# Attention scores from scaled fp16 halves in two sets, prepared one job ahead

## The chip, the cores and the metric

The kernel runs on one core of a Trainium2 chip. Its time is the device time of one execution in microseconds (us). TensorE (PE, its weight loads PEld) multiplies matrices, VectorE (DVE), ScalarE (ACT) and GpSimd (POOL) work on elements, and SyncE (SP) and ScalarE issue the DMA transfers of this kernel. Operands lie in SBUF, on 128 partitions; matmul results lie in PSUM.

## The reference

Attention of 8 batches with 8 heads, 576 positions and 64 columns a head, with a causal mask and a bias that falls with the running sum of max(s, 0); then a feed-forward network on the 4608 rows of 512:

```python
scores = 1.0 / np.sqrt(D) * np.matmul(q, k.transpose(0, 1, 3, 2))
cum = np.cumsum(np.maximum(s, 0.0), axis=-1)
bias = -(cum[:, :, :, None] - cum[:, :, None, :])
scores = np.where(causal, -1e9, scores + np.minimum(bias, 0.0))
attn = np.exp(scores - np.max(scores, axis=-1, keepdims=True))
attn = attn / (np.sum(attn, axis=-1, keepdims=True) + 1e-09)
x = np.matmul(attn, v)                      # then heads beside each other: 4608 x 512
h = x @ w_in                                # 512 x 2048
g = np.where(h >= 1, h, np.where(h <= -1, 0.0, (h + 1) ** 2 / 4.0))
out = g @ w_out                             # 2048 x 512
```

q, k, v and s are float32, and w_in and w_out float64. Both matter to the kernel: the weights are turned into pairs of fp16 numbers on the chip, and q and k are 8 times larger than a plain draw of 0.1 would be.

## The kernel before, in words

**Jobs.** Attention is cut into 64 jobs, each with two heads of one batch (a pair) and one half of the queries. HALF 0 has queries 0 to 320 and HALF 1 the other 256. A batch is 8 jobs: four pairs with half 0, then four with half 1. `att_slot(j, k)` emits job j in eight slots. Slot 0 prepares the operands (`att_prep`), slots 2 to 7 hold the job's six score tiles (`scores`), slot 3 loads the next job's q and k (`att_load`), and slot 7 multiplies the weights of the job before with v (`att_out`).

**Score operands.** `att_load` brings q and k, transposed, twice each: rows 0 to 63 and 64 to 127 of the tiles rq and rk get the same 64 columns of the head (four DMAs on SP, one buffer each). `att_prep` makes Q1 and K1 (q and k rounded to fp32r, a shorter float that TensorE takes as an operand) and Q2 and K2. Rows 64 to 127 of Q1 and rows 0 to 63 of K2 hold what rounding left, so that two matmuls give hi*hi + lo*hi + hi*lo. Rows 64 to 67 of Q2 and K2 carry the running sums in two parts against constant ones: thus the bias comes out of the same matmul (KC = 68 rows). Those rows are written by DMA from cumd, a copy of the running sums in HBM. There is one tile of each, Q1, K1, Q2 and K2, so a job's operands can be written only after the last score of the job before has read them.

**A job's chain.** The two matmuls of a score tile (L385, L386) fill one of two PSUM buffers of the tag "s". L391 (VectorE) adds the mask and takes the row minimum (scores are held negated), L402 (ScalarE) takes the exponential and its sum, L418 and L419 make the reciprocal, L423 to L426 and L429 (POOL, ScalarE, VectorE) make two fp16 halves pb of the normalised weights, and L430 transposes pb by DMA on SP into pt. Then `att_out` runs L448, the matmuls px of v's halves with pt, into a buffer of the same tag "s", and L459 and L460 make the fp16 halves of x.

**Feed-forward.** For each batch and half, 16 blocks ft of 128 hidden columns: 12 matmuls h (L502), the activation on ScalarE, VectorE and POOL (L514, L517, L518, L528, L529), and 12 matmuls y (L541) two blocks later. Four blocks go with one attention job, and attention runs about one half-batch ahead of the network, which needs x of all four pairs. At a boundary of two batches, job 8b+7's px must be done before the network can go on, and job 8b+8's operands are prepared.

**Start.** The float64 weights are decoded in 16 pieces each (`Weights.decode`, L193 to L204; `split` makes fp16 halves, L220 to L230). Those of w_in are decoded beside jobs 0 to 3, each in the four slots k = 0, 2, 4, 6; those of w_out while the network's first 16 blocks h run. v is scaled per batch in `batch_start`.

**Order.** The program is written in the loop order above, but a scheduler puts the instructions of each engine into one fixed order when the kernel is built, by priorities and its own estimate of times; `tc.high_priority` moves the score's minimum, the activations and x forward, and `late` and `issue_after` hold back the second half of pb. On the chip each engine goes through its order and waits for what is not ready. POOL makes K2 in the first 12 jobs (K_POOL), VectorE in the others.

## Time and profile before

| | |
|---|---|
| median of 3 runs | 1176.75 us (1176.42 to 1180.47) |
| profiled execution | 1170.07 us, span 1168.3 us |
| mean granted TensorE clock | 0.961 |
| TensorE busy | 1010.3 us, 86% |
| VectorE busy | 881.0 us, 75% |
| ScalarE busy | 744.6 us, 64% |
| POOL busy | 685.6 us, 59% |
| DMA moved | 158.04 MB, mean 135 GB/s |

The page's slices show how the kernel goes through its stages (40 slices of 29.2 us, tenths of busy time):

```profile
PE   1334677599998999889998999899989999899998
DVE  8988976778777877778777877788768777787633
ACT  5665686567746775667647765777557774777533
PEclk9997997599998999999999999999998999899999
```

TensorE fills up in the first eight slices and is then nearly full, with a step to 8 about every fourth slice: one step a batch. To read the rows: L385 is line 385 of the kernel before; an arrow shows out<-in; a bracket gives the idle time of the engine just before, and what ended it. A matmul's duration overlaps the next one's, so that starts are what can be subtracted.

### The profile page before, as it was taken

The page shows a single profiled execution, that of the slowest core. Times are in us where ns is not written, and L with a number is a line of the kernel's source. Part 1 is how long each engine was busy: PE and PEld are TensorE (multiplying, and loading weights), DVE is VectorE, ACT ScalarE, POOL GpSimd, SP SyncE. Part 2 cuts the span into 40 slices and gives each one's busy share as a digit, 9 for nine tenths or more (in the row PEclk, how much of TensorE's full clock was granted, in tenths as well). Part 3 has the DMA queues.
Part 4 walks back from the last instruction along what each step waited for, and adds up shares of the span by engine and source line. Part 5 has one row for each costly group of instructions (what it writes and reads, how often), then busy time and mean ns, then how long its engine had stood idle before and what let it go on. Part 6 is the DMA issues. An engine that isn't in the chain of part 4 may idle for free. (4 is left out here: it accounts for less than half of the span.)

```text
span 1168.3 us, 25129 instructions
## 1 busy us (share of the span) xinstructions
PE 1010.3 (86%) x8470; PEld 780.1 (67%) x8470; DVE 881.0 (75%) x2403; ACT 744.6 (64%) x1719; POOL 685.6 (59%) x1169
## 2 busy tenths in 40 slices
PE   1334677599998999889998999899989999899998
PEld 0222455477776877677776877677768877787787
DVE  8988976778777877778777877788768777787633
ACT  5665686567746775667647765777557774777533
POOL 4775247776546655565547664675647654775522
PEclk9997997599998999999999999999998999899999
DMA  8885316677528663677438753766537753667300
GB/s 256 210 190 154 121 58 151 153 149 159 140 75 182 155 160 83 124 155 166 118 86 177 152 145 83 166 145 156 120 93 167 163 139 78 156 141 160 79 27 19
DMA packets 343081, 158.04 MB, mean 135 GB/s; under 512 B 291112, under 2 KB 324264, under 8 KB 342952
## 3 DMA queue, kind: packets, MB, share of 16 engines
q1 hardware_dynamic: 334024, 147.26, 55.3%
q10 hardware_dynamic: 8928, 9.18, 2.5%
q8 instruction: 67, 1.10, 0.4%
q14 instruction: 62, 0.51, 0.2%
HBM read 75.33 MB, written 9.73 MB: 73 GB/s over the span
## 5 line engine op out<-in xcount | busy, mean ns | idle before, releaser
L502 PE MATMUL h<-x,WI 128*128 128x256 f16 (+1 forms) x3072 | 448.6, 291 | 24.3 <-DVE u L518 17.0
L541 PE MATMUL y<-g,WO 128*128 128x256 f16 (+1 forms) x3072 | 450.7, 290 | 9.9 <-POOL g L529 5.2
L502 PEld LDWEIGHTS <-WI 128*128 128x128 f16 x3072 | 292.7, 99 | 118.0 <-issue 28.4
L541 PEld LDWEIGHTS <-WO 128*128 128x128 f16 x3072 | 287.3, 99 | 99.4 <-issue 15.1
L529 POOL TENSOR_TENSOR g<-u,g 128x320 f16<-128x320 f32 (+1 forms) x256 | 204.4, 798 | 204.0 <-ACT g L528 198.6
L514 ACT ACTIVATE u<-h,ub,us 128x320 f32<-128x320 f32 (+1 forms) x256 | 150.2, 587 | 183.0 <-PE h L502 165.3
L402 ACT ACTIVATE p<-p,mn 64x64 f32<-64x64 f32 (+4 forms) x320 | 178.8, 559 | 107.2 <-DVE mn L391 82.2
L423 POOL TENSOR_SCALAR pb<-p,rs 64x128 f16<-64x128 f32 (+4 forms) x160 | 104.7, 655 | 167.4 <-DVE rs L419 117.8
L517 DVE SCALAR_TENSOR_TENSOR h<-h,ws,u 128x320 f32<-128x320 f32 (+1 forms) x256 | 132.5, 519 | 80.2 <-ACT u L514 80.1
L391 DVE CUSTOM_DVE_ANT_0 p<-s,mask 64x64 f32<-64x64 f32 (+4 forms) x320 | 135.1, 423 | 74.4 <-PE s L386 68.4
L385 PE MATMUL s<-K,Q 128*128 128x288 f32 (+4 forms) x384 | 151.2, 396 | 41.1 <-DVE mn L391 26.6
L429 DVE SCALAR_TENSOR_TENSOR pb<-p,rs,pb 64x128 f16<-64x128 f32 (+4 forms) x160 | 134.5, 841 | 52.4 <-POOL pb L423 52.0
L426 POOL TENSOR_TENSOR pb<-p,pb 64x128 f16<-64x128 f32 (+4 forms) x160 | 166.0, 1038 | 8.4
L386 PE MATMUL s<-K,Q 68*128 68x288 f32 (+4 forms) x384 | 121.3, 319 | 25.3 <-DMA K<-cumd 19.0
L518 DVE SCALAR_TENSOR_TENSOR u<-u,r,h 128x320 f32<-128x320 f32 (+1 forms) x256 | 130.2, 510 | 7.7 <-DVE h L517 0.5
L424 ACT ACTIVATE p<-p,rs 64x64 f32<-64x64 f32 (+4 forms) x160 | 89.4, 560 | 61.0 <-DVE rs L419 58.5
L528 ACT CAST g<-u 128x320 f16<-128x320 f32 (+1 forms) x256 | 108.4, 423 | 14.7 <-DVE u L518 14.5
L385 PEld LDWEIGHTS s<-K,Q 128*128 128x128 f32 (+1 forms) x384 | 74.6, 195 | 62.5 <-DVE mn L391 35.7
L448 PE MATMUL px<-pt,vt 128*64 128x256 f16 (+3 forms) x1536 | 89.0, 264 | 22.8 <-DMA pt<-pb 13.5
L448 PEld LDWEIGHTS <-vt 128*64 128x64 f16 x1536 | 75.8, 116 | 45.3 <-issue 32.4
L386 PEld LDWEIGHTS s<-K,Q 68*128 68x128 f32 (+1 forms) x384 | 76.1, 199 | 28.7 <-ACT x L459 10.1
L425 POOL TENSOR_SCALAR pb<-p 64x128 f16<-64x128 f32 (+4 forms) x160 | 91.2, 570 | 4.6 <-ACT p L424 2.0
(116 smaller groups left out, 954.6 us busy)
## 6 DMA issues: line engine op xcount, KB each, us to landing
rk<-in_k_dram SPq DMA_DIRECT2D x64, 288.0 KB
rq<-in_q_dram SPq DMA_DIRECT2D x64, 160.0 KB
rk<-in_k_dram SPq DMA_DIRECT2D x64, 160.0 KB
v<-in_v_dram SPq DMA_DIRECT2D x32, 288.0 KB
wir<-in_moe_w_in_dram SPq DMA_DIRECT2D x16, 512.0 KB
rq<-in_q_dram SPq DMA_DIRECT2D x64, 128.0 KB
wor<-in_moe_w_out_dram SPq DMA_DIRECT2D x16, 512.0 KB
out_dram<-o ACTq DMA_DIRECT2D x32, 160.0 KB
```

The costliest lines, as they stand in the source:

```text
L385: T.matmul(sc[:R, :c1 - c0], Q1[:, hd, qo:qo + R], K1[:, hd, c0:c1], start=True, stop=False)
L386: T.matmul(sc[:R, :c1 - c0], Q2[:KC, hd, qo:qo + R], K2[:KC, hd, c0:c1], start=False, stop=True)
L391: ttr[0] = V.tensor_tensor_reduce(out=Pt[:R, c0:c1], in0=sc[:R, :c1 - c0], in1=mask[:R, mo:mo + c1 - c0], scale=1.0, scalar=3.0e38 if mn i ...
L402: A.activation(Pt[:R, :W], Pt[:R, :W], AF.Exp, bias=m2[:R], scale=-1.0, accum_out=sums[n, i][:R, hd:hd + 1])
L426: G.tensor_tensor(los[1], pw, his[1], ALU.subtract)
L429: V.scalar_tensor_tensor(los[0], pv, rs[:R, :1], his[0], ALU.mult, ALU.subtract)
L448: T.matmul(px[hd * D:(hd + 1) * D, lo:N], VT[:, vl * NB + j, hd * D:(hd + 1) * D], PT[:, 4 * j + 2 * hd + pl, lo:], start=(m == 0), stop=( ...
L502: T.matmul(h[:, :N], WI[4 * kt + ft // 4][:, wl, ft % 4 * P:(ft % 4 + 1) * P], x[:, kt, xl], start=(n == 0), stop=(n == 3 * NKT - 1),)
L514: first = A.activation(u, h[:, :N], AF.Relu, bias=ubi[b], scale=usc[b]).ins
L517: V.scalar_tensor_tensor(h[:, :N], h[:, :N], wsc[b], u, ALU.mult, ALU.max)
L529: G.tensor_tensor(g[:, 1], u, g[:, 0], ALU.subtract)
L541: T.matmul(ys[b, hf, m][:, :N], WO[8 * (m // 2) + ft // 2][:, wl, c0:c0 + P], g[:, gl], start=(ft == 0 and n == 0), stop=(ft == NFT - 1 an ...
```

## The change

The score operands become fp16, in two sets that alternate by job, and a job's operands are prepared in slot 5 of the job before. fp16 has a small range, so q, k and the running sums are scaled by powers of two. For the running sums the power comes from their largest value (ctop, once). For q and k it comes, per batch, from a bound on what they can hold: each row's sum of magnitudes, taken by ScalarE (`scan`, an Abs with an accumulator) over q and k of the coming batch, which eight more loads per batch bring in (`scan_load`, 128x576 float32 each, on SP); `qk_scale` then takes the maximum over partitions with two transposes on TensorE, works out the factors in one-column operations on VectorE, and spreads them to all partitions with a matmul. `L465` divides the scale out again when it adds the mask. The running sums have three fp16 parts instead of two fp32r ones (NL = 3, KC = 70), and the constant rows beside them hold the scales (qkc), written by DMA in the first two jobs of each batch. The DMAs of these rows move from SP's queue to ScalarE's. Where POOL made K2, ScalarE now scales rk first.

```diff
-    LOADQ, CUMQ, FIRSTQ = nc.sync, nc.sync, nc.sync
+    LOADQ, CUMQ, FIRSTQ, SCANQ = nc.sync, nc.scalar, nc.sync, nc.sync
...
-    KC = D + 4
+    NL = 3
+    KC = D + 2 * NL
...
-    Q1 = cp.tile([P, 2, NQ], F32R, name="Q1")
-    K1 = cp.tile([P, 2, S], F32R, name="K1")
-    Q2 = cp.tile([P, 2, NQ], F32R, name="Q2")
-    K2 = cp.tile([P, 2, S], F32R, name="K2")
+    SETS = [
+        tuple(cp.tile([P, 2, m], F16, name=f"{t}_{i}") for t, m in (("Q1", NQ), ("K1", S), ("Q2", NQ), ("K2", S)))
+        for i in range(2)
+    ]
...
+    def scan_load(b, p):
+        for t, src in enumerate((qT, kT)):
+            raw = scans[b, p, t] = ap.tile([P, S], F32, tag="scan", bufs=2, name=f"sc{b}_{p}_{t}")
+            SCANQ.dma_start(raw, src[b, 2 * p:2 * p + 2].rearrange("h d n -> (h d) n"))
+    def scan(b, p):
+        if p == 0:
+            qkp[b] = ap.tile([P, 2, NPAIR], F32, tag="qkp", name=f"qkp{b}")
+        for t in range(2):
+            raw = scans.pop((b, p, t))
+            A.activation(raw, raw, AF.Abs, accum_out=qkp[b][:, t, p:p + 1])
+    def qk_scale(b):
+        t = ap.tile([P, 2], F32, tag="qkt", name=f"qkt{b}")
+        V.tensor_reduce(t, qkp.pop(b), axis=AX, op=ALU.max)
+        row = ps_s.tile([P, 512], F32, tag="s", name=f"row_qk{b}")
+        for i in range(2):
+            T.transpose(row[:1, i * P:(i + 1) * P], t[:, i:i + 1], ident)
...
+        V.tensor_reduce(qk, row[:1, :2 * P].rearrange("p (i n) -> p i n", i=2), axis=AX, op=ALU.max)
+        pow2floor(qk, qk, LEAST_QK)
...
+        col = ps_s.tile([P, 512], F32, tag="s", name=f"col_qk{b}")
+        T.matmul(col[:, :5], ones[:1], t16[:1], start=True, stop=True)
+        sc = qks[b] = ap.tile([P, 5], F32, tag="qks", name=f"qks{b}")
+        V.tensor_copy(sc, col[:, :5])
+        c = qkc[b] = ap.tile([NL, 2, S], F16, tag="qkc", bufs=1, name=f"qkc{b}")
+        for i in range(2):
+            G.tensor_scalar(c[:, i], ones16, sc[:NL, 3 + i:4 + i], 1.0, ALU.mult, ALU.mult)
...
     def att_prep(n, hf):
...
+        Q1, K1, Q2, K2 = SETS[j % 2]
...
+        if j % (2 * NPAIR) < 2:
             for hd in range(2):
+                CUMQ.dma_start(K2[D:D + NL, hd], qkc[b][:, 0])
+                CUMQ.dma_start(Q2[D + NL:KC, hd], qkc[b][:, 1, :NQ])
+        CUMQ.dma_start(Q2[D:D + NL, :, :N], cd[:, :, q0:W])
+        CUMQ.dma_start(K2[D + NL:KC, :, :W], cd[:, :, :W])
+        A.activation(Q1[:, :, :N], rq, AF.Copy, scale=sq)
+        A.activation(K1[:, :, :W], rk, AF.Copy, scale=sk)
+        A.activation(Q2[:D, :, :N], rq[:D], AF.Copy, scale=sq[:D])
+        V.scalar_tensor_tensor(Q1[D:, :, :N], rq[D:], sq[D:], Q1[D:, :, :N], ALU.mult, ALU.subtract)
+        if j in K_POOL:
+            A.activation(rk[:D], rk[:D], AF.Copy, scale=sk[:D])
+            G.tensor_tensor(K2[:D, :, :W], rk[:D], K1[:D, :, :W], ALU.subtract)
         else:
+            V.scalar_tensor_tensor(K2[:D, :, :W], rk[:D], sk[:D], K1[:D, :, :W], ALU.mult, ALU.subtract)
...
-            if k == 0:
-                att_prep(n, hf)
...
+            i = j % (2 * NPAIR) - SCAN_J
+            b = j // (2 * NPAIR) + 1
+            if k == SCAN_K and b < B:
+                if 0 <= i < NPAIR:
+                    scan_load(b, i)
+                if 1 <= i <= NPAIR:
+                    scan(b, i - 1)
+                if i == NPAIR + 1:
+                    qk_scale(b)
+            if k == PREP_K and j + 1 < len(jobs):
+                att_prep(*jobs[j + 1])
...
+    for p in range(NPAIR):
+        scan_load(0, p)
+        scan(0, p)
     att_load(0, 0)
+    qk_scale(0)
+    att_prep(0, 0)
```

The fixed order of each engine changes with it, at three places that the prediction speaks of. The first is TensorE's, where batch 2 ends and batch 3 begins: from the last score tile of job 23 (s_4_1_288, its K and Q) to its px (the last row). Before, with the middle left out: s_4_1_288_5848 and the group px_1_5862 of job 22, then the first scores of job 24, then job 23's px_1_6121:

```order
L385 MATMUL s_4_1_288_5848<-K_90,Q_89 128x288
L386 MATMUL s_4_1_288_5848<-K_92,Q_91 128x288
L541 LDWEIGHTS WO_130
L541 MATMUL y_0_1_5308<-g_0_12_5927,WO_130 128x320
L448 LDWEIGHTS vt_4545
L448 MATMUL px_1_5862<-pt_1_5486,vt_4545 64x256
...
L385 MATMUL s_2_1_0_6107<-K_90,Q_89 128x320
L386 MATMUL s_2_1_0_6107<-K_92,Q_91 128x320
L448 LDWEIGHTS vt_4815
```

In the rows left out stand 28 matmuls y, 30 h, one px group of 30 and job 24's six score pairs. The same place in the changed kernel:

```order
L459 MATMUL s_4_1_288_6132<-K_1_94,Q_1_93 128x288
L460 LDWEIGHTS Q_1_95
L460 MATMUL s_4_1_288_6132<-K_1_96,Q_1_95 128x288
L585 LDWEIGHTS WI_133
L585 MATMUL h_1_0_6454<-x_1_5644,WI_133 128x256
L522 LDWEIGHTS vt_4774
...
L459 MATMUL s_2_1_0_6395<-K_0_90,Q_0_89 128x320
L460 LDWEIGHTS Q_0_91
L460 MATMUL s_2_1_0_6395<-K_0_92,Q_0_91 128x320
L522 LDWEIGHTS vt_5050
```

Here 12 matmuls y, 13 h, one px group of 30 and the same six pairs stand between: 33 feed-forward matmuls fewer.

The second is SP's order of transfers at the same place; pt_1_5722 (before) and pt_1_5995 (after) are job 23's transposed weights, made in two parts (i = 3 and 4), and vt is a later job's transposed v. Before:

```order
L430 DMA_TRANSPOSE pt_1_5722<-pb_3_5723 128x16x128
L333 DMA Q_91<-cumd 2x2x320
L334 DMA K_92<-cumd 2x2x320
L317 DMA rq_0_5996<-in_q_dram 64x2x320 x2
L317 DMA rk_0_5997<-in_k_dram 64x2x320 x2
L430 DMA_TRANSPOSE pt_1_5722<-pb_4_5854 128x20x128
L430 DMA_TRANSPOSE pt_0_5987<-pb_0_5988 128x4x64
L363 DMA_TRANSPOSE vt_6045<-vb_5934 128x10x128
```

After:

```order
L504 DMA_TRANSPOSE pt_1_5995<-pb_3_5996 128x16x128
L388 DMA rk_0_6541<-in_k_dram 64x2x320
L388 DMA rq_0_6540<-in_q_dram 64x2x320 x2
L388 DMA rk_0_6541<-in_k_dram 64x2x320
L436 DMA_TRANSPOSE vt_6322<-vb_6211 128x10x128
L504 DMA_TRANSPOSE pt_1_5995<-pb_4_6138 128x20x128
L504 DMA_TRANSPOSE pt_0_6264<-pb_0_6265 128x4x64
```

The DMAs from cumd have left SP, and the transpose of v has moved from behind job 23's second pt transpose to ahead of it.

The third is VectorE's order at the start, where the first score tile is read. Before:

```order
L194 TENSOR_SCALAR WO_127,peak_wi<-WO_127 128x512
L258 TENSOR_SCALAR rc_171<-rc_171 128x4
L110 TENSOR_REDUCE top_m_185<-row_m_183 1x1
L195 TENSOR_SCALAR WO_127<-WO_127 128x512
L116 CAST t_m_187<-top_m_185 1x1
L203 SCALAR_TENSOR_TENSOR WO_127<-wir_201,WO_127 128x512
L194 TENSOR_SCALAR WO_128,peak_wi<-WO_128 128x512
L119 COPY mb_182<-col_m_189 128x1
L391 ISA p_0_0_225,mn_0_0_0_230<-s_0_0_0_227,mask 64x64
```

After:

```order
L214 TENSOR_SCALAR WO_158,peak_wi<-WO_158 128x512
L372 COPY qks_233<-col_qk_231 128x5
L116 TENSOR_REDUCE top_m_273<-row_m_271 1x1
...
L223 SCALAR_TENSOR_TENSOR WO_158<-wir_639,WO_158 128x512
...
L224 SCALAR_TENSOR_TENSOR WO_158<-wir_639,WO_158 128x512
L286 RECIPROCAL mr_280<-mb_270 128x1
L288 TENSOR_SCALAR ex_282<-c_258,mr_280 128x4
L465 ISA p_0_0_304,mn_0_0_0_309<-s_0_0_0_306,mask,qks_233 64x64
```

WO_127 and WO_128 hold the fourth and fifth decoded pieces of w_in, WO_158 the fourteenth: the first score tile is now read behind 14 decoded pieces instead of five, and behind the scales of batch 0 (qks).

71 lines of the change are left out of this document (46 added, 25 removed).

## The prediction

> **What bounds the kernel now.** I read the page's engine totals first, then the same totals by stage, because an average over the span hides that the stages have different limits.
>
> ```profile
> PE 1010.3 (86%) x8470; PEld 780.1 (67%) x8470; DVE 881.0 (75%) x2403; ACT 744.6 (64%) x1719; POOL 685.6 (59%) x1169
> core 0: us, PE busy (x) PEld busy (x) DVE busy (x) ACT busy (x) POOL busy (x), PEclk, DMA share, GB/s
> 20.00:96.00 76.00, 27.44 (x141) 18.39 (x141) 65.59 (x189) 51.09 (x112) 52.81 (x84) 0.99 0.85 209
> 96.00:163.00 67.00, 42.28 (x265) 26.60 (x264) 57.00 (x126) 40.78 (x67) 26.54 (x27) 0.88 0.32 102
> 163.00:246.00 83.00, 59.18 (x410) 43.16 (x410) 58.65 (x171) 53.25 (x118) 57.47 (x84) 0.75 0.60 139
> 246.00:1100.00 854.00, 816.26 (x7075) 637.78 (x7073) 659.27 (x1834) 566.75 (x1361) 523.01 (x934) 0.98 0.61 136
> ```
>
> The reader should see four regimes. From 20 to 96 us (weights decoded beside jobs 0 to 3) TensorE works a third of the time and VectorE and the DMA are the limit. From 96 to 163 VectorE is busy 57.0 of 67. From 163 to 246 no engine is full: attention latency shows. From 246 on TensorE is busy 816.26 of 854, so 38 us are lost there in all. They are lost where one batch ends and the next begins, six times. This is one such place, TensorE's timeline after the last scores of job 31:
>
> ```profile
> 601.69 0.30 PE L386 MATMUL s<-K,Q 68*128 68x288 f32 x1
> 602.07 1.51 PE L448 MATMUL px<-pt,vt 128*64 128x256 f16 x30
> 603.94 1.79 PE L502 MATMUL h<-x,WI 128*128 128x320 f16 x12
> 605.57 1.11 PE L541 MATMUL y<-g,WO 128*128 128x320 f16 x7
> 613.41 1.51 PE L448 MATMUL px<-pt,vt 128*64 128x256 f16 x30 [0.54 <-DMA pt<-pb]
> 617.52 0.21 PE L386 MATMUL s<-K,Q 68*64 68x64 f32 x1 [2.42 <-DMA K<-cumd]
> PE s L386 <- DMA K<-cumd: 19.0, 8, 4.5
> PE px L448 <- DMA pt<-pb: 13.5, 13, 2.0
> ```
>
> Job 31's last score ends at about 602.0, its weighted sum px can start at 613.4. That 11.7 us chain is covered by other matmuls up to the last 0.54 us. Then the first scores of job 32 wait 2.42 us, because its K tile is written only now; the last two rows are the whole run's sums, 19.0 us in 8 such waits and 13.5 in 13 waits of px. The chain's links, from the same window's other engines and queues:
>
> ```profile
> 603.79 0.76 ACT L402 ACTIVATE p<-p,mn 128x576 f32<-128x576 f32 x1
> 605.33 0.78 ACT L424 ACTIVATE p<-p,rs 128x576 f32<-128x576 f32 x1 [0.33 <-DVE rs L419]
> 607.01 1.40 POOL L426 TENSOR_TENSOR pb<-p,pb 128x640 f16<-128x640 f32 x1
> 607.92 1.17 DVE L429 SCALAR_TENSOR_TENSOR pb<-p,rs,pb 128x640 f16<-128x640 f32 x1
> 611.18 0.80 DVE L361 SCALAR_TENSOR_TENSOR vb<-v,rc,vb 128x576 f16<-128x576 f32 x1
> 609.15 4.32 SPq L430 DMA_TRANSPOSE pt<-pb  x2
> 613.56 1.28 SPq L363 DMA_TRANSPOSE vt<-vb  x1
> ```
>
> Exponential, normalising, splitting into halves, transposing by DMA: the transposes alone take 4.32 us from 609.15. The next job's vt transpose comes after them, when it delays nobody.
>
> **The change part by part.** All sums are against the profiled execution, 1170.07 us (span 1168.3); the median of the runs shown, 1176.75, is 0.57% above it, so 6.7 us are added at the end.
>
> *Scores in fp16.* The pair's price is read where TensorE runs without a gap:
>
> ```profile
> 492.90 0.71 PE L541 MATMUL y<-g,WO 128*128 128x320 f16 x4
> 493.34 0.41 PE L385 MATMUL s<-K,Q 128*128 128x320 f32 x1
> 493.59 0.30 PE L386 MATMUL s<-K,Q 68*128 68x320 f32 x1
> 493.74 1.49 PE L502 MATMUL h<-x,WI 128*128 128x256 f16 x12
> ```
>
> Durations overlap, so I take starts. Twelve fp16 matmuls of 320 columns go from 603.94 to 605.57 (quoted above): 0.136 each. Four of them and the pair go from 492.90 to 493.74, 0.84; so the pair costs 0.84 - 4 x 0.136 = 0.30, where two fp16 matmuls would cost 0.27. That is 0.03 us saved. There are 64 x 6 = 384 pairs, some 324 of them in jobs that run where TensorE is the limit: -10 us. Bounds: 0 (starts this close could hide it) to 0.08 a pair, which is more than a quarter of its price, -26.
>
> *The batch boundary.* Two edits work here, and one would help. Two sets and a preparation one job earlier write K long before job 32's scores, so the 2.42 us wait should go. But what stands between the last scores and px moves. The order of instructions (shown ahead) has, between the last scores of job 23 and its px, 28 y, 30 h and 30 px matmuls with 6 score pairs before, and 12 y, 13 h, 30 px and 6 pairs after. At 0.136 (h and y; some have 256 columns, so a little less) and 1.51 us for the px group that is 58 x 0.12 + 1.5 + 6 x 0.3, about 10.3 before, and 25 x 0.12 + 1.5 + 1.8 = 6.3 after. The static order cannot shift work into the gap when the chain is late. And the chain gets longer: ScalarE now has two DMA issues, x and a part of the next preparation between the exponential and the normalising, and on SP the next job's vt transpose (1.28 us) and its wait for L434 on VectorE (0.80, the row of 611.18) stand ahead of the critical pt transposes. I take 11.7 + 2.5 = 14.2. That is an estimate from the two rows and the places in the order, not a measured chain. The px wait becomes 14.2 - 6.3 = 7.9 instead of 0.54, and 2.42 is given back: +4.9, and for six boundaries, of whose orders I followed one in full, +30. Bounds: a chain that stays at 11.7 gives 5.4 - 0.54 - 2.42 = 2.4, +15 in all; a chain of 16 gives 6.7, +40.
>
> The gap's second price is the clock:
>
> ```profile
> 610.00:620.00 10.00, 5.60 (x60) 4.37 (x58) 6.83 (x24) 7.07 (x20) 6.30 (x13) 1.00 0.78 185
> 620.00:624.00 4.00, 3.88 (x17) 2.55 (x17) 4.00 (x14) 1.89 (x9) 2.71 (x6) 0.57 0.81 148
> ```
>
> After 4.4 idle us in ten, the granted clock is 0.57 for the next four. One such dip stands at the boundary already; a longer gap can widen it by up to a few us each, 0 to +10 in all, and I put nothing into the sum. The Trainium skill, "TensorE: Matmul & The Clock Gate", Part 1: The HAM clock gate, has a rule that speaks against the change here: an idle window of some 3.4 us drops TensorE to half clock, and about as much busy time brings it back. By that rule a gap of 7.9 us holds one or two whole idle windows where today's pieces of 0.5 and 2.4 us hold at most one by chance, and by an estimate from the page's window each boundary would lose up to 1.7 us more, +10; the row of 620 agrees that such a window exists.
>
> *Batch scales.* Each batch adds two PE transposes, a 1x128 matmul and about 18 one-column VectorE operations between them, and both score buffers are held meanwhile (row_qk and col_qk). One such operation:
>
> ```profile
> 601.85 0.15 DVE L288 TENSOR_SCALAR ws<-us 128x1 f32<-128x1 f32 x1
> ```
>
> 18 x 0.15 = 2.7 us plus what queues between; the order has 8 us of y and h matmuls in that place, so the chain is covered, and I charge only TensorE's own instructions, about 0.4 us in each of seven batches: +3. If the chain takes longer than its cover, 2 us a batch, +14; below, 0.
>
> The sums of magnitudes are 64 ScalarE passes over 128x576. No row shows one; nearest is the exponential with its accumulator read:
>
> ```profile
> L402 ACT ACTIVATION_READ_ACCUMULATOR p<-p,mn 128x1 f32 x256 | 48.6, 190 | 0.0
> 21.21 0.20 DVE L391 CUSTOM_DVE_ANT_0 p<-s,mask 64x64 f32<-64x64 f32 x1
> 75.31 0.47 PE L386 MATMUL s<-K,Q 68*128 68x320 f32 x1
> 92.51 0.94 PE L448 MATMUL px<-pt,vt 128*64 128x320 f16 x18 [1.97 <-DMA pt<-pb]
> L194 DVE TENSOR_SCALAR_CACHE_REDUCE WO<-WO 128x512 f32<-128x512 f32 x32 | 21.7, 679 | 9.9 <-ACT WO L193 9.7
> L195 DVE TENSOR_SCALAR WO<-WO 128x512 int32<-128x512 int32 x32 | 19.1, 598 | 0.2
> L203 DVE SCALAR_TENSOR_TENSOR WO<-wir,WO 128x512 int32<-128x512 int32 x8 | 7.2, 895 | 0.0
> ```
>
> 0.76 + 0.19 = 0.95 each, 61 us in all. From 246 on ScalarE is 66% busy, and that absorbs its 36 passes at no cost; if it did not, boundaries would pay, which the chain's bound of 16 holds. The other 28 fall earlier.
>
> *Start, 0 to 96.* VectorE reads the first scores at 21.21 today, after 5 weight decodes; in the new order after 14 and after the first batch's scales. Nine decodes more at 0.68 + 0.60 + 0.90 = 2.2 are 20 us, the scales 3 to 5, and eight loads of 128x576x4 bytes, 2.4 MB, at the stage's 209 GB/s 11 more of DMA time that partly overlaps: first scores at about 50. Jobs 0 to 3 then took 75.31 - 21.21 = 54 us beside the decodes; with two decodes left, but rq and rk still single and ScalarE carrying an extra pass per job for POOL's subtraction, I take 11 us a job: last scores near 95, px not at 92.5 but near 108. Part of the 16 is made up, since the decodes are done sooner: +12 (6 to 20).
>
> *96 to 163.* ScalarE's 40.8 of 67 gets up to 20 of the passes, 19 us: 89% busy beside VectorE's 85%. +4 (0 to 14).
>
> *163 to 246.* The sets let a job's Q and K be made while the last one's scores run, in the stage where latency shows; but 24 us of ScalarE work from the passes and the extra pass make its 53.3 of 83 about 90%. I take 0 (-12 to +8).
>
> cum's third part and the wider 70-row contraction add no matmul. Its DMAs move from SP to ScalarE's queue; that costs ScalarE two issues a job, counted in the chain. No cost else.
>
> Sum: -10 + 30 + 3 + 12 + 4 + 0 = +39, so 1209 profiled and, with 6.7, **1216 us** as a median.
>
> **The rivals.** *Faster, the preparation pays.* With Q and K ready, the chain's engines have less in front of exponential and splits, and it shortens. The point is a chain of 6.3 + 0.54 + 2.42 = 9.3 us: below it the boundary gains. With 9.3 there, -10 for fp16, -10 from 163 to 246 where the clock of 0.75 also recovers, and +10 for the start, scales and the rest together: 1160, median 1167. For it: the 19.0 us of K waits do go. Against: the links quoted sum to 0.76 + 0.78 + 1.40 + 1.17 + 4.32 = 8.4 without any wait between them.
>
> *Slower still: ScalarE and SP in step at the start.* Scan tiles have two buffers, and their loads stand in SP's order among w2's. When a pass waits for its load, every exponential and relu behind it on ScalarE waits, and SP's next load waits for the buffer. At 2 to 3 us for each of about 16 passes up to 246, +35 instead of +16: 1228, median 1235, and up to 1245 with the clock.
>
> *No net change.* A chain of 11.7 (+15), the full -26 of fp16, 0 for the scales and +6 and +4 for the start: 1169, median 1176.
>
> *The change doesn't do what it says:* fp16 scores cost as much per column as before (0.136 x 2 against 0.30 leaves little to gain anyway). Then -10 is 0: 1226.
>
> **How the numbers follow.** Forecast 0.50, preparation pays 0.18, in step 0.16, no net change 0.08, no fp16 gain 0.08. About 0.5% is what a measurement of this kernel tells from no change. Faster is the second case, 0.18; same the fourth, 0.08; slower the rest, 0.74. The forecast's own range is 1196 to 1236 (boundary 15 to 40 and start 6 to 20, not all at their ends together). For eight in ten I reach to the faster case's edge, 1166, and to 1244.
>
> **What would show it.** Right: a wait of px for pt of 5 to 10 us at each of six boundaries (13.5 us in all now, 2.0 the longest), no wait on K from cumd, first scores read near 50, the score pair at 0.27. Wrong: px waits of under 3 us at the boundaries, or a stage from 163 to 246 shorter by 10 us or more; then the job-ahead preparation was worth more than the order's thinner cover.

## The result: slower, and by twice the forecast

The changed kernel takes 1252.61 us (median of 4 runs, 1251.41 to 1255.38) against 1178.61 for the kernel before: a ratio of 1.0629 with a 95% interval of 1.0606 to 1.0653. The direction was forecast; +74 us was not (+39), and the time lies above the range.

The engine totals of the changed kernel, and the sums of what TensorE waited for over the whole run:

```profile
PE 1005.2 (80%) x8496; PEld 753.7 (60%) x8496; DVE 941.4 (75%) x2557; ACT 814.2 (65%) x1859; POOL 684.2 (55%) x1184
PE px L522 <- DMA pt<-pb: 58.6, 17, 7.6
PE s L459 <- DVE mn L465: 41.6, 48, 3.1
PE y L624 <- POOL g L612: 11.9, 18, 2.2
```

The wait of px for pt is 58.6 us where it was 13.5; the wait of the scores for K from cumd (19.0) is gone. VectorE has 60 us more work and ScalarE 70.

Where does it come from in time? Each kernel is cut at the px of jobs 15 and 55: the part ahead of it holds the start and one batch boundary, the part between is five whole batches, and the rest is the end. The same view for the five batches, before and then after:

```profile
355.50:998.50 643.00, 611.02 (x5292) 476.83 (x5293) 494.80 (x1386) 424.25 (x1021) 389.94 (x701) 0.98 0.61 137
```

```profile
406.30:1079.60 673.30, 611.65 (x5307) 465.23 (x5309) 531.12 (x1473) 438.80 (x1036) 396.03 (x711) 0.96 0.61 133
```

px of job 15 starts 50.8 us later (406.3 against 355.5), five batches take 30.3 us more, 6.1 each, and the end takes as long as before (169.9 against 169.8). So the spans differ by 81.2, and the medians by 74.0: the profiled execution of the kernel before took 1170.07 us, 8.5 less than the median of its runs, so that up to some 7 us of what follows is that one execution. TensorE is busy as long as before in the five batches (611.65 against 611.02); the whole 30 us are idle time. The waits of the same five batches, before:

```profile
PE s L386 <- DMA K<-cumd: 13.5, 6, 2.6
PE px L448 <- DMA pt<-pb: 7.0, 8, 1.7
PE s L385 <- DVE mn L391: 6.5, 14, 0.9
PE y L541 <- POOL g L529: 4.1, 4, 2.2
```

and after:

```profile
PE px L522 <- DMA pt<-pb: 35.7, 9, 6.3
PE s L459 <- DVE mn L465: 19.3, 19, 2.8
PE y L624 <- POOL g L612: 9.1, 12, 2.2
```

One boundary on TensorE's timeline, after job 31's last score (which ends at 659.6):

```profile
664.79 0.25 PE L460 MATMUL s<-K,Q 70*128 70x192 f16 x1
667.61 0.30 PE L459 MATMUL s<-K,Q 128*128 128x320 f16 x1 [2.58 <-DVE mn L465]
668.74 0.30 PE L459 MATMUL s<-K,Q 128*128 128x320 f16 x1 [0.69 <-DVE mn L465]
674.50 2.77 PE L522 MATMUL px<-pt,vt 128*64 128x256 f16 x30 [5.33 <-DMA pt<-pb]
```

and SP's transposes in the same window:

```profile
668.36 1.27 SPq L436 DMA_TRANSPOSE vt<-vb  x1
669.73 4.07 SPq L504 DMA_TRANSPOSE pt<-pb  x2
```

This is much of the picture that the prediction drew: vt first, then the critical pt, and a px that waits 5.33 us and then runs on half the clock (0.50 granted from 674.5 to 677.3; 30 matmuls in 2.77 us, 1.51 before). The 2.58 and 0.69 us in which the scores wait for the minimum are not in it.

The stages of the start, after:

```profile
0.00:49.10 49.10, 1.62 (x7) 0.54 (x7) 40.75 (x107) 29.55 (x47) 12.15 (x24) 1.00 0.96 300
49.10:119.50 70.40, 21.39 (x122) 11.89 (x122) 45.24 (x140) 51.13 (x123) 41.86 (x78) 1.00 0.83 198
119.50:195.60 76.10, 47.38 (x292) 29.73 (x292) 62.39 (x132) 56.41 (x110) 28.46 (x29) 0.84 0.54 169
195.60:279.90 84.30, 47.96 (x330) 30.20 (x330) 62.12 (x181) 59.74 (x130) 48.96 (x75) 0.76 0.71 155
```

The rows are cut at the first score, px of job 3, the first score of job 4 and px of job 8. In the kernel before these stand at 19.7, 92.5, 162.8 and 241.2 us: the lateness is 29, 27, 33 and 39 us, and it goes on growing to 51 at px of job 15.

### The profile page after: what moved, and what is told of

Its sections match the earlier page's. It is cut to its first block, busy times and chain, and to the rows that moved or that the text cites. A ratio compares the mean times of both kernels' runs of the same rounds, so it can differ in the third digit from the quotient of the medians.

```text
span 1249.5 us, 25524 instructions
## 1 busy us (share of the span) xinstructions
PE 1005.2 (80%) x8496; PEld 753.7 (60%) x8496; DVE 941.4 (75%) x2557; ACT 814.2 (65%) x1859; POOL 684.2 (55%) x1184
## 3 DMA queue, kind: packets, MB, share of 16 engines
q1 hardware_dynamic: 342464, 165.31, 58.6%
## 4 chain that ended last, share of the span: by engine, by line
PE 46%; DMA 15%; DVE 14%; POOL 10%; ACT 7%; issue 6%; SPq 1%; ACTq 0%; DVEq 0%; POOLq 0%
PE y L624 19%; PE h L585 19%; DMA pt<-pb 5%; PE px L522 4%; POOL pb L500 3%; DVE pb L503 2%; POOL pb L497 2%; PE s L459 2%; DMA wor<-in_moe_w_out_dram 2%; DMA sc<-in_k_dram 2%; DVE p L465 2%; DMA vt<-vb 2%; PE s L460 2%; POOL g L612 2%; DMA out_dram<-o 2%
## 5 line engine op out<-in xcount | busy, mean ns | idle before, releaser
L585 PEld LDWEIGHTS <-WI 128*128 128x128 f16 x3072 | 302.2, 99 | 132.6 <-issue 36.6
L624 PEld LDWEIGHTS <-WO 128*128 128x128 f16 x3072 | 295.9, 98 | 111.7 <-issue 22.2
L612 POOL TENSOR_TENSOR g<-u,g 128x320 f16<-128x320 f32 (+1 forms) x256 | 196.4, 767 | 193.7 <-ACT g L611 193.4
L465 DVE CUSTOM_DVE_ANT_0 p<-s,mask,qks 64x64 f32<-64x64 f32 (+4 forms) x320 | 152.8, 482 | 63.7 <-PE s L460 55.2
L459 PE MATMUL s<-K,Q 128*128 128x288 f16 (+4 forms) x384 | 111.5, 294 | 50.2 <-DVE mn L465 41.6
L522 PE MATMUL px<-pt,vt 128*64 128x256 f16 (+3 forms) x1536 | 95.4, 278 | 63.4 <-DMA pt<-pb 58.6
L522 PEld LDWEIGHTS <-vt 128*64 128x64 f16 x1536 | 81.8, 123 | 89.3 <-issue 50.5
L460 PE MATMUL s<-K,Q 70*128 70x288 f16 (+4 forms) x384 | 112.1, 295 | 13.5 <-POOL K L413 13.5
L460 PEld LDWEIGHTS <-Q 70*128 70x128 f16 (+1 forms) x384 | 39.8, 104 | 70.9 <-issue 62.3
L408 ACT ACTIVATE K<-rk,qks 128x640 f16<-128x640 f32 (+1 forms) x64 | 66.0, 1031 | 11.0 <-DMA rk<-in_k_dram 11.0
```

The costliest lines, as they stand in the source:

```text
L459: T.matmul(sc[:R, :c1 - c0], Q1[:, hd, qo:qo + R], K1[:, hd, c0:c1], start=True, stop=False)
L460: T.matmul(sc[:R, :c1 - c0], Q2[:KC, hd, qo:qo + R], K2[:KC, hd, c0:c1], start=False, stop=True)
L465: ttr[0] = V.tensor_tensor_reduce(out=Pt[:R, c0:c1], in0=sc[:R, :c1 - c0], in1=mask[:R, mo:mo + c1 - c0], scale=qks[n // NPAIR][:R, 2:3], ...
L522: T.matmul(px[hd * D:(hd + 1) * D, lo:N], VT[:, vl * NB + j, hd * D:(hd + 1) * D], PT[:, 4 * j + 2 * hd + pl, lo:], start=(m == 0), stop=( ...
L585: T.matmul(h[:, :N], WI[4 * kt + ft // 4][:, wl, ft % 4 * P:(ft % 4 + 1) * P], x[:, kt, xl], start=(n == 0), stop=(n == 3 * NKT - 1),)
L612: G.tensor_tensor(g[:, 1], u, g[:, 0], ALU.subtract)
```

## The experiments

All times are medians; the kernel before had 1175.8 to 1178.6 in the groups of runs. Every edit also gives the engines a new fixed order, so that each run measures its edit together with the order that came of it.

### Part of the change at a time

**row_in_h**: the scale chain's row and column out of the score buffers.

```diff
-        row = ps_s.tile([P, 512], F32, tag="s", name=f"row_qk{b}")
+        row = ps_h.tile([P, 512], F32, tag="h", name=f"row_qk{b}")
...
-        col = ps_s.tile([P, 512], F32, tag="s", name=f"col_qk{b}")
+        col = ps_h.tile([P, 512], F32, tag="h", name=f"col_qk{b}")
```

> The change as it is, except that the row and the column of the batch scales (row_qk, col_qk) take a buffer of the network's h in PSUM instead of one of the two score buffers. Theory A (the scales' chain holds the score buffers, so the scheduler puts the feed-forward work elsewhere and only 25 of its matmuls are left between job 8b+7's last score and its px, 58 before): in this build 106 stand there, so the px waits of 5 to 6 us at the six boundaries are gone, and the time falls by 6 x 6 = 36 us to about 1215 us. Rival B (the chain itself is longer, because ScalarE and SP carry more): px waits stay, time above 1240. Either way the start stays some 40 us late.

Measured 1263.61, ratio 1.0745 (1.0711 to 1.0779). The px waits did go, and other waits came:

```profile
PE h L585 <- DVE u L601: 20.7, 7, 4.4
PE y L624 <- POOL g L612: 17.4, 28, 2.4
PE s L459 <- DVE mn L465: 10.4, 20, 1.2
PE px L522 <- DMA pt<-pb: 5.0, 6, 1.9
```

The cover at the boundary (the matmuls that stand between a batch's last score and its px) is not the cause by itself: with 106 of the network's matmuls in the gap instead of 25 five batches take 685.9 us. The chain now holds one of the network's two h buffers, and the network waits.

**scales_once**, **scales_const** and **f16_alone** leave out more and more. For scales_once the later batches' branch is off and they share batch 0's scales; for scales_const there is no chain:

```diff
+    def qk_const():
+        sc = one = ap.tile([P, 5], F32, tag="qks", bufs=1, name="qks")
+        for i, value in enumerate((-32.0, 32.0, 2.0 ** -13, 64.0, -64.0)):
+            V.memset(sc[:, i:i + 1], value)
...
-            if k == SCAN_K and b < B:
+            if False:
```

f16_alone also has one set, `att_prep(n, hf)` back in slot 0 and `CUMQ = nc.sync`.

> Sums of magnitudes and scales for batch 0 only; the other batches use its scales (they are equal for these inputs), so 56 loads, 56 ScalarE passes and seven scale chains are left out. Theory A: the order has 58 feed-forward matmuls at the boundary again; time about 1210 us, close to row_in_h, since the passes themselves cost little after 246 us. Rival C (the passes and loads cost time of their own all along, 0.95 us of ScalarE each): 20 us or more below row_in_h, so below 1195.

> No sums of magnitudes and no scale chain at all: the five scales are constants (the values that the chain finds). fp16, two sets, the preparation a job ahead and ScalarE's queue stay. Theory D (the late start comes from the first batch's loads, passes and scale chain ahead of the first score): first score read near 20 us again, and the time is 35 to 44 us below scales_once, about 1170. Rival E (it comes from the operands: the extra ScalarE pass per job, two sets, the preparation's new place): less than 15 us below scales_once, about 1200.

> Of the change only the fp16 operands with constant scales and the three-part sums: one set, each job's preparation in its own slot 0, the sums' DMAs on SP. By the price read from the trace (0.30 against 0.27 us a score pair) 10 us faster than before: 1168. Rival (no gain from fp16 scores): 1178. Rival (a pair gains up to 0.08): 1153.

scales_once: 1213.66, ratio 1.0315 (1.0288 to 1.0342), close to the 1210 of theory A, though not for its reason (see below). scales_const: 1206.11 (1.0226 to 1.0289): only 7.5 less, rival E; the first batch's loads and chain are a small part of the late start. f16_alone: 1226.68, ratio 1.0432 (1.0397 to 1.0466): none of the three expectations. It still has the scales in columns, the run-time scale of the sums and the extra ScalarE pass, and with these fp16 operands were 50 us slower than before; two sets, the preparation a job ahead and the sums' DMAs on ScalarE's queue were together worth 20 us.

### What the fp16 operands bring with them

The rows of the score minimum and of two ScalarE copies, before, and in f16_alone:

```profile
L391 DVE CUSTOM_DVE_ANT_0 p<-s,mask 128x448 f32<-128x448 f32 x64 | 39.7, 621 | 39.9 <-PE s L386 39.7
L326 ACT ACTIVATE Q<-rq 128x640 fp32r<-128x640 f32 x32 | 23.6, 737 | 6.4 <-PE s L385 6.4
L335 ACT CAST K<-rk 128x640 fp32r<-128x640 f32 x32 | 22.8, 714 | 0.0
```

```profile
L475 DVE CUSTOM_DVE_ANT_0 p<-s,mask,qks 128x448 f32<-128x448 f32 x64 | 43.5, 680 | 28.4 <-PE s L470 28.4
L417 ACT ACTIVATE Q<-rq,qks 128x640 f16<-128x640 f32 x32 | 26.2, 819 | 4.6 <-PE s L469 4.6
L418 ACT ACTIVATE K<-rk,qks 128x640 f16<-128x640 f32 x32 | 26.0, 814 | 0.0
```

The inputs now name qks: the scale is read from a column of SBUF. The minimum takes 59 ns longer, and 64x64 tiles too (0.211 to 0.271), so it is a fixed price per instruction; the copies take 82 and 100 ns longer. Three runs on this:

```diff
-                scale=qks[n // NPAIR][:R, 2:3], scalar=3.0e38 if mn is None else mn[:R],
+                scale=2.0 ** -13, scalar=3.0e38 if mn is None else mn[:R],
...
-        A.activation(K1[:, :, :W], rk, AF.Copy, scale=sk)
+        A.activation(K1[:, :, :W], rk, AF.Copy, scale=32.0)
```

(and the other five operands likewise) is const_literal, on scales_const. const_sums, on scales_const, does the same to the sums' scale alone and takes the first rows from SBUF:

```diff
-    crow = ps_s.tile([P, 512], F32, tag="s", name="crow")
...
-    V.tensor_scalar(cum[:BH], cum[:BH], cinv[:BH], 2.0 ** 14, ALU.mult, ALU.mult)
+    V.tensor_scalar(cum[:BH], cum[:BH], 128.0, None, ALU.mult)
```

f16_sums_literal has both, on f16_alone.

> scales_const with the running sums' scale a constant too (no maximum, transpose and matmul for it ahead of the fp16 parts), and the first two jobs' rows of sums sent from SBUF as in the kernel before instead of through HBM. In scales_const the first score is still read at 33 us against 20 before. Theory F (the sums' own chain makes that late, and it is carried to the end): first score near 20, time 10 to 14 us below scales_const, about 1194. Rival G (the other lateness of the start swallows it: weights and single q and k buffers pace jobs 0 to 3 anyway): under 4 us, above 1202.

> scales_const with every scale written into the instruction as a number instead of read from a column (score minimum, the ScalarE copies, the halves on VectorE). In the traces the minimum of 128x448 takes 0.68 us with the column and 0.62 in the kernel before, the copy of 128x640 0.82 against 0.74. Theory H (these 0.06 to 0.10 us are the operand's price, and since score buffers wait for the minimum they cost time): durations return to 0.62 and 0.74, the batches get 1 to 1.5 us shorter, time 8 to 15 us below scales_const. Rival (the durations come from fp16 or from load elsewhere): durations stay, time as scales_const, 1206.

> f16_alone with constant sums' scale, the first two jobs' sums from SBUF, and all scales written into the instructions: what is left of the change are fp16 operands and a third part of the sums. If the sums' chain at the start and the column operands are all that made f16_alone 50 us slower, this is 1177 less up to 7 for fp16 scores: 1170. Rival (fp16 operands cost something of their own, for instance 64-column score tiles, whose pair takes 0.27 us between two feed-forward matmuls against 0.09 before): above 1190.

const_sums: 1208.36, ratio 1.0275 (1.0244 to 1.0306), no gain: rival G. Its first score comes at 21.4 us instead of 33.1, and px of job 3 at 102.8 instead of 103.2. **An earlier first score bought nothing.** const_literal: 1193.97, ratio 1.0145 (1.0117 to 1.0174), 12 us less, theory H, with the minimum back at 621 ns and the copies at 732 and 724 (so a column costs a copy 87 to 90 ns; the other 10 of the 100 come from the instruction, which was a cast before). The batches got 0.7 us shorter, where 1 to 1.5 were expected:

```profile
L475 DVE CUSTOM_DVE_ANT_0 p<-s,mask 128x448 f32<-128x448 f32 x64 | 39.7, 621 | 25.5 <-PE s L470 23.8 <-POOL p L465 1.0
L417 ACT ACTIVATE Q<-rq 128x640 f16<-128x640 f32 x32 | 23.4, 732 | 17.6 <-DMA K<-qkc 6.4 <-PE s L469 6.2 <-DMA rq<-in_q_dram 5.1
```

f16_sums_literal: 1192.51, ratio 1.0139 (1.0112 to 1.0166), 34 us less than f16_alone. It is the rival's time that holds there, since 16 us remain; part of its reason can be read from the trace (64-column tiles, below), and the extra ScalarE pass is still in this run.

The same price put alone into the kernel before, before_columns (five operands, these two among them; of the two halves on VectorE only Q's has a scale):

```diff
-        A.copy(K1[:, :, :W], rk)
+        A.activation(K1[:, :, :W], rk, AF.Copy, scale=cols[:, 1:])
...
-                scale=1.0, scalar=3.0e38 if mn is None else mn[:R],
+                scale=cols[:R, 1:], scalar=3.0e38 if mn is None else mn[:R],
```

> The kernel before, its scales (-0.125 and 1) read from a column instead of written into the instructions: the score minimum, the three ScalarE copies, the two halves on VectorE. No fp16, no sets. Theory H (columns cost 0.06 to 0.10 us each and the score buffers wait for them): minimum of 128x448 at 0.68 instead of 0.62, and 12 to 25 us slower, about 1195. Rival (the kernel before hides them): within 5 us, 1180.

1201.82, ratio 1.0220 (1.0186 to 1.0254): 26 us, with no fp16 in it. Five of its batches:

```profile
367.90:1024.70 656.80, 621.17 (x5290) 482.07 (x5291) 514.79 (x1386) 436.88 (x1023) 389.41 (x701) 0.97 0.63 134
```

Against the kernel before: 13.8 us more, of which idle is only 3.6; TensorE is busy 10.2 us longer for the same matmuls. Most of that is the clock: summed over 2 us windows, the busy time lost to a granted clock below 1 is 19.8 us, 11.1 before. These are one execution each, and the mean clock of the kernel before was 0.947 to 0.965 from run to run (0.961 in its profile, 0.949 in this one), so the size of this part is uncertain. The order changed as well: VectorE's differs from the one before at many places, mostly by neighbours that changed places. The 26 us are what the columns cost with the order that came of them.

The part of the change that sends the sums by ScalarE's queue, alone in the kernel before (`CUMQ = nc.scalar`):

> The kernel before with one part of the change alone: the sums' DMAs leave SP for ScalarE's queue. Theory I (the wait of the first scores for K, 19.0 us in all, comes from these DMAs standing behind the weights' transposes in SP's order): the wait goes, 10 to 17 us faster than before, about 1164. Rival J (the wait has another reason, the last reader of K, or the issues on ScalarE lengthen the chain by as much): within 4 us of before, 1177.

1177.94, ratio 1.0010 (0.9989 to 1.0031). The wait of the scores for K from cumd is gone from its list, and

```profile
PE px L448 <- DMA pt<-pb: 19.8, 13, 5.1
PE y L541 <- POOL g L529: 9.5, 8, 2.2
```

stand at 19.8 and 9.5 instead of 13.5 and 5.2. The cause of theory I was right and its gain wrong, rival J. That these two waits took the place of the one that went is likely and not shown: this profile is of an execution of 1181.18 us, and the one before of 1170.07.

### Scale chain, loads and passes apart

chain_only, chain_passes and chain_loads put back what scales_once leaves out, one part each:

```diff
+    def fixed(b):
+        qkp[b] = ap.tile([P, 2, NPAIR], F32, tag="qkp", name=f"qkp{b}")
+        V.memset(qkp[b], 288.0)
...
-                if 0 <= i < NPAIR:
-                    scan_load(b, i)
-                if 1 <= i <= NPAIR:
-                    scan(b, i - 1)
                 if i == NPAIR + 1:
+                    fixed(b)
                     qk_scale(b)
```

> The change without the later batches' loads and sums of magnitudes (batch 0 keeps its own); each later batch still makes its scales, from a constant 288 in place of the sums. Between scales_once (1214, no chain either) and the change (1253) lie 39 us. Theory K (the chain costs the boundaries, the loads and passes cost the start, where the fixed order puts 32 of these 56 passes): the batch period stays near 134.6, px of job 15 comes near 390 instead of 406, time about 1236. Rival L (it is all the chain): 1250. Rival M (loads and passes cost the batches too): period near 131, below 1222.

> As chain_only, with the 56 ScalarE passes kept, over a tile that holds a constant 0.5 (sum 288), and only the loads left out. Theory K1 (ScalarE's 0.95 us a pass is what the start pays): px of job 15 near 402, time about 1248. Rival K2 (the loads' place among the weights' on SP and their HBM traffic pay): as chain_only, 1236.

> As chain_only, with the 56 loads kept, and of each pass only one column (so that its tile comes free). Theory K1 (passes): as chain_only, about 1236. Rival K2 (loads): px of job 15 near 402, about 1248.

chain_only 1239.01, ratio 1.0516 (1.0495 to 1.0537); with the passes 1246.86 (1.0558 to 1.0608); with the loads 1249.00 (1.0582 to 1.0631). Over scales_once the chain costs 25 us: five batches go from 656.0 to 675.1 us, and VectorE's work in them from 511.0 to 530.1, in chain_only:

```profile
385.40:1041.40 656.00, 606.04 (x5290) 462.01 (x5290) 511.00 (x1386) 435.07 (x1020) 385.06 (x701) 0.97 0.64 134
393.10:1068.20 675.10, 613.32 (x5307) 465.76 (x5308) 530.07 (x1474) 434.14 (x1020) 395.36 (x711) 0.95 0.61 130
```

Passes add 8, loads 10, both together (the change) 14. Theory K holds for the chain; between K1 and K2 the runs say both, and px of job 15 shows that they act at the start (393.1, then 402.8 and 399.2, and 406.3 in the change). In the change's trace 48 of the 64 passes run before 246 us and 56 before px of job 15.

fewer_ahead lets fewer of them go into the start:

```diff
-            qkp[b] = ap.tile([P, 2, NPAIR], F32, tag="qkp", name=f"qkp{b}")
+            qkp[b] = ap.tile([P, 2, NPAIR], F32, tag="qkp", bufs=1, name=f"qkp{b}")
```

(the same for qkt)

> The whole change, with one buffer instead of two for the sums and for their maxima (qkp, qkt), so that the scheduler can pull only 16 passes and loads of later batches into the start instead of 32; the other 40 fall behind, 8 a batch. Theory K: px of job 15 some 8 us earlier, time about 1243, if the batches absorb their passes. Rival M: the batches get longer by what the start gains, 1250 or above.

1255.32, ratio 1.0662 (1.0639 to 1.0685): px of job 15 is 2.5 us earlier and the batches 1.1 us longer. Rival M.

chain_mid_batch moves the chain away from the boundary:

```diff
-            b = j // (2 * NPAIR) + 1
+            b = j // (2 * NPAIR) + 2
...
-                if i == NPAIR + 1:
-                    qk_scale(b)
+            if k == 1 and j % (2 * NPAIR) == 2 and b - 1 < B:
+                qk_scale(b - 1)
```

> The whole change, with every batch's scale chain made at job 8b+2 of the batch before instead of 8b+6 (sums of magnitudes one batch further ahead). The order has 58 feed-forward matmuls at the boundary again instead of 25. Theory A2 (the chain's place next to the boundary is what costs the 3.5 to 3.8 us a batch between scales_once and chain_only): period 131 to 132 instead of 134.6, time 1228 to 1235. Rival N (wherever the chain stands, it takes its two score buffers and the same time from the network, as row_in_h took h's): period 134 or more, time above 1246.

1255.29, ratio 1.0687 (1.0645 to 1.0730), five batches 673.1: rival N. The 58 matmuls were back in the gap, px still waited 4.0 to 5.7 us at each boundary, and the cost stayed:

```profile
PE px L522 <- DMA pt<-pb: 26.1, 11, 5.7
PE s L459 <- DVE mn L465: 13.7, 24, 1.2
PE y L624 <- ACT g L611: 6.4, 10, 1.5
```

### What is left of fp16, and the network's lag

literal_k_vector is const_literal with `K_POOL = ()`: no extra ScalarE pass and no POOL subtraction in the first 12 jobs.

> const_literal with K2 made by VectorE in all jobs, so that the extra ScalarE pass and POOL's subtraction of the first 12 jobs are gone. const_literal's px of job 3 comes at 100.7 us, before's at 92.5. Theory O (the extra pass in front of POOL makes these jobs late): px of job 3 near 95, 5 us or more faster than const_literal, below 1189. Rival P (VectorE is the limit there and gets 0.9 us a job more): not faster, 1194 or above.

1190.66, ratio 1.0120 (1.0093 to 1.0148). px of job 3 comes at 96.2 instead of 100.7 and px of job 15 at 362.3 instead of 369.4: theory O at the start, 3 us in the time where 5 were asked. In the batches y waits for the network's own activations:

```profile
PE y L634 <- POOL g L622: 20.3, 17, 2.5
PE px L532 <- DMA pt<-pb: 12.6, 9, 2.9
```

(five batches). The last three runs have `Y_LAG = 3` for 2, in this kernel, in the one before, and in the change.

> literal_k_vector with y three blocks behind h instead of two (Y_LAG = 3); 74 feed-forward matmuls stand at the boundary instead of 58. Theory Q (y's wait for POOL's g is the lag's): this wait, 23.6 us in five batches, falls below 8, and the time by 15 to 20 us to about 1172. Rival R (the wait only shows that attention sets the pace): another wait takes its place, 1186 or above.

> The kernel before with Y_LAG = 3. Its wait for g is 5 us in five batches and its px waits 6.4. Theory Q: 5 to 10 us faster, about 1169. Rival R: within 4 us of before.

> The change with Y_LAG = 3: at the boundary 37 to 42 feed-forward matmuls instead of 25. By the boundary's arithmetic in the prediction 12 to 17 matmuls of 0.12 us cover 1.5 to 2 us more of the px wait: 9 to 12 us faster for six boundaries, about 1242. Rival N (attention sets the pace, so a cover only moves the wait): within 4 us of 1253.

literal_lag3: 1162.33, ratio 0.9869 (0.9853 to 0.9886), 28 us less. The wait for g is not in its list at all; the largest in five batches is

```profile
PE s L469 <- DVE mn L475: 17.4, 13, 3.6
```

and these batches take 628.9 us, 14 less than before. before_lag3: 1160.95, ratio 0.9851 (0.9836 to 0.9866), 17 us faster than the kernel before; theory Q had 5 to 10. The two are the fastest of all the runs, and their intervals overlap. after_lag3: 1237.26, ratio 1.0509 (1.0486 to 1.0532), 15 us less than the change where 9 to 12 were expected. So a wider lag pays in every version, and with it the change stays 76 us behind the kernel before.

## Why the prediction was right or wrong

The forecast had +39 us and the medians say +74. In medians the runs go from 1177 to 1194 (const_literal), 1206 (scales_const), 1214 (scales_once), 1239 (chain_only) and 1253 (the change): 17 us for fp16 operands and two sets, 12 for scales in columns, 8 for the first batch's loads, passes and scales, 25 for the later batches' scale chains, 14 for their loads and passes (76 together, since the groups of runs differ by a few us). Each step holds its part with the fixed order that came of it.

A ledger of the five batches: idle time, busy time, the busy time lost to the clock (summed over 2 us windows of the profile, 1 minus the granted clock times busy), and what remains as TensorE's own work at full clock; with it, px of job 15, which carries the start.

| kernel | px of job 15 | five batches | idle | lost to clock | work |
|---|---|---|---|---|---|
| before | 355.5 | 643.0 | 32.0 | 11.1 | 599.9 |
| before_columns | 367.9 | 656.8 | 35.6 | 19.8 | 601.4 |
| f16_alone | 386.9 | 668.2 | 51.2 | 16.8 | 600.2 |
| f16_sums_literal | 366.8 | 649.9 | 40.0 | 12.4 | 597.5 |
| const_literal | 369.4 | 651.9 | 45.9 | 12.3 | 593.7 |
| scales_const | 376.6 | 655.6 | 45.9 | 15.3 | 594.4 |
| scales_once | 385.4 | 656.0 | 50.0 | 12.0 | 594.0 |
| chain_only | 393.1 | 675.1 | 61.8 | 16.8 | 596.5 |
| after | 406.3 | 673.3 | 61.6 | 14.5 | 597.1 |
| before_lag3 | 354.4 | 637.4 | 28.6 | 12.5 | 596.3 |

**fp16 pairs, -10: right for the pair that was read, not shown for the sum.** From the start of the matmul ahead of a pair of 320 columns to the start of the one behind it, on a full clock and without a gap, it is 0.415 us before and 0.385 in the change (medians of 35 and 32 places): 0.03 saved, as read. The pairs of 192, 288 and 448 columns save 0.02 to 0.04. But the pair of 64 columns, one of the six of a job, takes 0.384 instead of 0.200 there (20 and 22 places), which would give back what the others save. Over 240 pairs work falls by nothing in f16_alone and by 2.4 to 6.2 us in the other runs with fp16, while before and before_lag3, with the same matmuls, differ by 3.6.

**The boundary, +4.9 each: near in size, partly by luck.** The batches grew by 6.1 us. The wait for K from cumd went, px waits for pt 5 to 6 us at each boundary (7.9 forecast), and from the last score to px it is 15.1 to 16.2 us (14.2 estimated, 16 the bound; these and the 11.7 before count from the last score's start, where the prediction says its end). Of the 38 us that the prediction saw lost at six boundaries, 24 lie there in the trace of the kernel before (from 13 us ahead of such a px to 8 behind it). And the argument "a thinner cover, hence a wait" fell. row_in_h and chain_mid_batch restore the cover and win nothing. And scales_once and scales_const have the 58 matmuls of the kernel before in the gap and no later chain, and px still waits 4.6 to 5.0 us at every boundary. What grew is the way to px: 15.7 to 16.2 us from the last score's end in these two runs, 11.4 to 12.3 before. SP and px after job 31's last score in scales_const, where vt goes first:

```profile
630.55 1.27 SPq L446 DMA_TRANSPOSE vt<-vb  x1
631.92 4.70 SPq L514 DMA_TRANSPOSE pt<-pb  x2
637.14 2.77 PE L532 MATMUL px<-pt,vt 128*64 128x256 f16 x30 [4.61 <-DMA pt<-pb]
```

and in const_literal, whose fixed order has vt behind pt:

```profile
625.82 4.31 SPq L514 DMA_TRANSPOSE pt<-pb  x2
630.18 1.40 SPq L446 DMA_TRANSPOSE vt<-vb  x1
631.71 1.86 PE L532 MATMUL px<-pt,vt 128*64 128x256 f16 x30 [3.12 <-DMA pt<-pb]
```

There it is 12.3 to 13.3 us and px waits 2.1 to 3.1. So the prediction's longer chain with vt ahead of pt fits, and the cover does not. The two runs also differ in the columns, and no run parts the order from the columns. It also means that the 12 us between them are not the price of the columns alone.

**Batch scales, +3 with 14 as the bound: this step failed.** The prediction held the chain to be covered by other matmuls and charged TensorE's own instructions. The chain measured 25 us (scales_once to chain_only): 3.8 us a batch, wherever it stood, and 7.7 up to px of job 15, one boundary in it. VectorE has 3.8 us more work a batch (2.7 was the estimate for the one-column operations), and at the boundary the scores now wait 2.58 and 0.69 us for its minimum (above). Whether this work is the cause, or the two score or h buffers that the chain takes from the others, or the constant rows that are written again in each batch, is not shown: each fits all three placings, and no run parted them.

**"No cost else": this step failed too.** The description of the change shows the scales of L465 and of the copies as columns; the prediction has no term for them and no reason why not. Read from a column they are 59 to 90 ns longer. before_columns: 26 us in the kernel before. In the change's company it is 12 us (const_literal against scales_const); why less is not shown. For ScalarE the Trainium skill says as much ("ScalarE: Activation LUTs", What ACT_TABLE_LOAD costs): an activation with its scale as a number is cheaper, and every column operand adds about 93 ns; the copies agree with 87 and 90. For the minimum on VectorE the traces alone give 59.

**The start, +12, +4 and 0: mis-sized; it measured +45** (50.8 less a boundary of 6). The prediction had the first scores at 50 and the last of job 3 near 95, and they came at 49.1 and 97.1. But px of job 3, forecast near 108, came at 119.5: it stood 22 us behind the last scores, where the forecast had 13 and the kernel before has 17. And the prediction counted on the lateness being made up after that, and it grew. The steps up to px of job 15, in us: fp16 with literal scales, sums' parts and two sets +6.8 (literal_k_vector); the extra ScalarE pass and POOL's subtraction of the first 12 jobs +7.1; scales from columns +7.2; batch 0's loads, passes and scales +8.8; the later batches' chains +7.7, one boundary in it; their loads and passes +13.2. Together 50.8. The prediction put the last item at 4, because it had 28 of the 64 passes ahead of 246 us and 36 in the stage where ScalarE would absorb them. In the trace of the change 48 run ahead of 246 us and 16 behind, the last at 497. The extra pass it counted in its 11 us a job for jobs 0 to 3, and after that it set it off against the gain of the sets. In these stages the busiest engine has 73 to 82% (rows above), and added work still makes the jobs later, though not by its length: the later batches' 48 passes ahead of px of job 15, 0.87 us each or 42 in all, made it 9.7 us later (chain_only to chain_passes). The first score itself was a bad mark: const_sums moved it by 11.7 us and nothing followed.

**The clock, 0 with +10 as the bound.** In the change 3.4 us more are lost to it in five batches; in before_columns 8.7 (one execution each). The half clock comes in multiples of 3.4 us in the clock records of the trace. That is the window in the rule of the Trainium skill ("TensorE: Matmul & The Clock Gate", Part 1: The HAM clock gate). The direction was right and the estimate of +10 too high for the change: the half clock stands 59 us in its five batches, 24 before, but most of the added time falls on idle.

**The rivals.** "ScalarE and SP in step at the start" came nearest, in its number alone: +35 there, 1235 to 1245, from 2 to 3 us a pass. ScalarE did wait for the passes' loads, but 20.4 us in 23 waits over the whole run, 0.9 each; the later passes and loads cost the start 13 us, as one cause of six. "The preparation pays" is true of its part in one comparison: two sets, the earlier preparation and the sums on ScalarE's queue gain 20 us between f16_alone and scales_const, both with scales from columns; with literal scales the two designs are level (1192.5 and 1194.0).

**The signs.** All four signs of being right came: px waits of 5 to 6 us at the boundaries, no wait for K from cumd, first scores at 49.1, and a pair of 320 columns at 0.276 us. None of them watched the scale chain, the columns or the stages behind the first scores, where the missing time lay.

What stays open: where literal_k_vector's 14 us over before come from, beyond y's wait for g, which a lag of three ended, and the 64-column pairs; the mechanism of the chain's 3.8 us; and how much of each step is the fixed order that came with it. A general version of the fp16 kernel needs scales that are found at run time, and none was found that beats the kernel before. before_lag3, one number changed, is the version to keep.

## What to carry to other kernels

Price an operand, not only an instruction: here a scale that moved from the instruction into a column cost a fixed time in every use, and hundreds of uses added up. In stages where no engine is full, a busy share does not say that added work is free, and a mark such as the first score need not be on the chain that sets the time. Look in the fixed order for where added instructions really stand before giving them to a stage. A wait that is moved away is not a gain until the sum of all waits falls; and before work is added to buy slack, try the constant that sets it.

## What the hardware showed that was not expected

A column operand adds 59 ns to a masked minimum on VectorE (0.211 to 0.271 at 64x64, 0.621 to 0.680 at 128x448) and 87 to 90 ns to a ScalarE copy of 128x640. A pair of fp16 matmuls of 64 columns takes 0.18 us longer between two of the network's matmuls than the fp32r pair, while the wider pairs take 0.02 to 0.04 less. In five batches 3.6 us more of idle time came with 8.7 us more lost to the clock (before_columns, one execution each). And one block more of lag between two matmul stages was worth 15 to 28 us in three different kernels, though the wait that it was aimed at was 4 to 20 us in five batches; in the kernel before these waits fell by about 1 us of 4, so that they are not where its 17 us came from.
